# Bias bands of four heads read from one SBUF partition each instead of a copy in HBM

## The chip, the cores and the metric

The kernel runs on one core of a Trainium2 chip. The metric is the device time of one execution in microseconds (us), as the median of several runs. The core's engines work side by side, each through its own list of instructions in order: PE (matrix products, with PEld for loading weights), DVE (vector operations), ACT (exponential, copies, activations), POOL and SP. POOL and SP here mostly issue DMA transfers; each has a queue of its own, which all 16 DMA engines of the core serve (q0 in the profile is POOL's queue, q1 SP's). SBUF is the memory on the chip with 128 partitions, PSUM the one that PE writes to, HBM the memory outside.

## The reference

Attention with a relative position bias, then a feed-forward layer. There are 8 batches, 8 heads, 576 positions and 64 numbers per head:

```python
scores = scale * np.matmul(q, k.transpose(0, 1, 3, 2))
# n = abs(i - j); bucket(n) is n up to 15, then logarithmic, the last of 32 from 128 on
scores = scores + bias_table[bucket].transpose(2, 0, 1)[None]
attn = softmax(scores)
x = (attn @ v)            # to (4608, 512)
h = x @ w_in              # (512, 2048)
out = np.maximum(0.01 * h, h) @ w_out
```

The bias depends on the distance |i - j| and the head alone, and is constant from distance 128 on. A constant drops out of the softmax. So only a band of the scores about the diagonal needs the bias at all, and the kernel multiplies there by exp(bias - last bias) after the exponential.

## The kernel before

The work is cut into 32 items, one for each batch and pair of heads (`items`, n = 0 to 31; item n < 4 is pair n of batch 0). For an item, Q and K are loaded by POOL's queue, transposed (by PE for the early items), copied to SBUF by DVE or ACT (`qt`, `kt`), multiplied by PE in six parts u (`qk_mm`, scores in `ps_s`), put through the exponential by ACT (`exp`, to `at` and `at4`), multiplied by the band by DVE (`band`), multiplied with V by PE (`av...`, `ps_o`), divided and laid out for the feed-forward layer, whose products fill PE's remaining time and everything after the last item.

For the first eight items the order of all steps on all engines is written out by hand in a table, `first`, of which these lines are the start:

```python
spin 9 o, tq 0, cq 0 a, tk 0, ck 0, ap 0, spin 2 o,
begin 0, m 0 0, m 0 2, tk 1, tq 1, e 0 0, m 0 1, ck 1, e 0 2, m 0 5, e 0 1, e 0 5, m 0 4 s, m 0 3,
e 0 4, spin 3 m, cq 1 v, ap 1, e 0 3, m 1 0, tk 2, b 0 5, ck 2, b 0 1, e 1 0, m 1 1, ap 2, m 1 2,
e 1 1, b 0 0, b 0 4, m 1 4, tq 2,
begin 1, e 1 4, spin 3 m, m 1 3, b 0 2, e 1 2, b 1 0, cq 2 v, at 0, ...
```

Here `tk n` and `tq n` are PE's transposes of pair n's K and Q (L292), `ck`, `cq ... v` and `ap` DVE's copies of them (L313, L307, L299), `m n u` PE's scores of part u (L347 to L358), `e n u` ACT's exponential (L373 to L385), `b n u` DVE's band (L408, and L401 for `b 0 5`), `at n` and `ac n ...` PE's products with V, `dv` the division, and `spin` products of ones (L1041) whose result nobody reads. Each engine keeps the order of its own steps.

The band is made once, at the start. `ub` is a tile of 8 partitions, one for each head, with 512 numbers (bf16): exp(bias - last bias) laid out by distance, the same to both sides. `hk` holds for each head 128 partitions of 384 numbers, where partition i is the head's row read from number i on. That is a row fetched 128 times, shifted by one number each time. `hk4` is the same for the last 64 positions, 192 numbers wide, for all pairs. Before the change, SP stores `ub` to HBM (`u_row`, L202) and then fetches from there: heads 0 and 1, heads 2 and 3 (`load_hk`, L204), `hk4` in two halves (`load_hk4`, L211), heads 4 and 5, heads 6 and 7. Item p of batch 0 uses heads 2p and 2p + 1; `b 0 5` reads `hk`, since `hk4` comes later, and the parts 5 of all other items read `hk4`.

Of the kernel before, what the change touches and what calls it, by code (L numbers as in the profile page):

```python
# [37 lines left out]
def kernel(  # L38
# [10 lines left out]
    nc = tc.nc  # L49
# [6 lines left out]
    P = 128  # L56
# [33 lines left out]
    hk = per.tile([P, H, 3 * P], BF16, name="hk")  # L90
# [83 lines left out]
    BW = 3 * P  # L174
    ub = per.tile([H, UW], BF16, name="ub")
# [15 lines left out]
    for j, (u, lo, w, m) in enumerate(groups):  # L191
        copy = nc.scalar.copy if j % 2 else nc.vector.tensor_copy
        copy(out=ub[:, C0 + lo : C0 + lo + m * w].rearrange("h (m w) -> h m w", w=w),
             in_=e8[:, u : u + m].unsqueeze(2).to_broadcast([H, m, w]))
    row = ub[:, :]
    nc.vector.tensor_copy(
        out=ub[:, C0 - BAND + 1 : C0],
        in_=bass.AP(tensor=row.tensor, offset=row.offset + C0 + BAND - 1,
                    ap=[list(row.ap[0]), [-1, BAND - 1]]),
    )  # L200
    udr = nc.dram_tensor("u_row", [H, UW], BF16, kind="Internal")
    nc.sync.dma_start(out=udr.ap(), in_=ub)  # L202
    def load_hk(h0, h1):
        nc.sync.dma_start(  # L204
            out=hk[:, h0:h1, :],
            in_=bass.AP(tensor=udr, offset=h0 * UW, ap=[[1, P], [UW, h1 - h0], [1, BW]]),
        )

    def load_hk4(p0, p1):
        for e in range(2):  # L210
            nc.sync.dma_start(  # L211
                out=hk4[e * SL : (e + 1) * SL, p0:p1, :],
                in_=bass.AP(tensor=udr, offset=(2 * p0 + e) * UW + SL + P,
                            ap=[[1, SL], [2 * UW, p1 - p0], [1, P + SL]]),
            )

    load_hk(0, 2)
    load_hk(2, 4)
    load_hk4(0, n_pairs)
    load_hk(4, 6)  # L220
    load_hk(6, H)
# [1091 lines left out]
```

## Time and profile before

| | |
|---|---|
| median of 3 runs | 366.75 us (366.44 to 367.57) |
| the profiled execution | 365.69 us, span 363.9 us |
| PE, ACT, DVE, POOL busy | 98%, 67%, 52%, 29% of the span |
| mean granted TensorE clock | 0.995 |
| `hk` transfers, from issue to landing | 4.8 to 9.6 us, median 6.9 us |
| DVE idle until the first `hk` is there | 3.0 us, once |

The span is the time from the first instruction to the last; the execution's own time lies 1.8 us above it. Rows in order of time begin with the start in us from the span's start and the length in us. What stands in brackets is the idle time ahead of a row and what ended it. A row with x2 or more stands for several instructions in succession, some with other shapes than the first, which is the one named. Rows of a queue (SPq, POOLq, ACTq) are issues of DMAs: their length is that of the issue, not of the transfer. The rows of DMA issues end with KB each and the us from issue to landing. The rows of queues give packets, MB and the time of the packets as a share of 16 engines; packets overlap, so the share can pass 100%.

### The profile page before, as it was taken

The page shows a single profiled execution, that of the slowest core. Times are in us where ns is not written, and L with a number is a line of the kernel's source. Part 1 is how long each engine was busy: PE and PEld are TensorE (multiplying, and loading weights), DVE is VectorE, ACT ScalarE, POOL GpSimd, SP SyncE. Part 2 cuts the span into 40 slices and gives each one's busy share as a digit, 9 for nine tenths or more (in the row PEclk, how much of TensorE's full clock was granted, in tenths as well). Part 3 has the DMA queues.
Part 4 walks back from the last instruction along what each step waited for, and adds up shares of the span by engine and source line. Part 5 has one row for each costly group of instructions (what it writes and reads, how often), then busy time and mean ns, then how long its engine had stood idle before and what let it go on. Part 6 is the DMA issues. An engine that isn't in the chain of part 4 may idle for free.

```text
span 363.9 us, 12095 instructions
## 1 busy us (share of the span) xinstructions
PE 356.2 (98%) x5195; PEld 207.4 (57%) x5195; DVE 189.1 (52%) x499; ACT 243.8 (67%) x363; POOL 106.6 (29%) x195
## 2 busy tenths in 40 slices
PE   7899999999999999999999999999999999999996
PEld 3465555555557776666666666666666544444443
DVE  4698777686755767555555666556554300100000
ACT  5899987479958888777777777777776264054111
POOL 8857427253334334423343334211000000000000
PEclk9899999999999999999999999999999999999999
DMA  7999999998998899988998799765411000200212
GB/s 100 189 195 155 192 205 160 196 136 128 99 128 137 107 153 125 140 130 118 134 117 135 115 118 131 122 105 95 51 49 50 29 31 0 86 31 0 86 60 86
DMA packets 105852, 40.27 MB, mean 111 GB/s; under 512 B 83648, under 2 KB 101320, under 8 KB 105800
## 3 DMA queue, kind: packets, MB, share of 16 engines
q0 software_dynamic: 55200, 18.36, 47.9%
q1 hardware_dynamic: 49304, 19.06, 27.0%
q10 hardware_dynamic: 1296, 2.10, 1.6%
q8 instruction: 41, 0.67, 0.8%
q14 instruction: 11, 0.09, 0.1%
HBM read 37.68 MB, written 9.45 MB: 130 GB/s over the span
## 4 chain that ended last, share of the span: by engine, by line
PE 89%; POOL 2%; ACT 2%; DMA 2%; DVE 1%; issue 1%; ACTq 0%; POOLq 0%
PE pm L843 35%; PE pm L584 16%; PE pm L532 14%; PE ps_o L476 8%; PE ps_s L354 7%; PE pm L718 2%; DMA kn<-in_k_dram 2%; PE ps_o L432 1%; PE ps_o L421 1%; PE ps_s L843 1%; ACT at L373 1%; POOL vn L137 1%; PE pm L577 1%; PE ps_s L347 1%; POOL qn L124 1%
## 5 line engine op out<-in xcount | busy, mean ns | idle before, releaser
L373 ACT ACTIVATE at<-ps_s 128x1024 bf16<-128x1024 f32 x120 | 118.5, 1023 | 34.1 <-PE ps_s L354 33.3
L843 PE MATMUL pm<-xT,w_in_sb 64*128 64x512 bf16 x608 | 139.6, 376 | 0.0
L843 PE MATMUL pm<-w_out_sb,gt 64*128 64x512 bf16 x544 | 129.6, 376 | 0.0
L556 ACT ACTIVATE gt<-pm 128x512 bf16<-128x512 f32 x140 | 82.2, 606 | 39.8 <-PE pm L532 33.9
L408 DVE TENSOR_TENSOR at<-at,hk 128x768 bf16<-128x768 bf16 (+3 forms) x149 | 64.8, 452 | 35.6 <-ACT at L385 21.4
L843 PEld LDWEIGHTS <-w_in_sb 64*128 64x128 bf16 x608 | 51.9, 94 | 23.9 <-issue 1.2
L843 PEld LDWEIGHTS <-gt 64*128 64x128 bf16 x544 | 48.3, 94 | 20.8 <-issue 0.7
L584 PE MATMUL pm<-w_out_sb,gt 128*128 128x512 bf16 x268 | 59.8, 380 | 0.0
L532 PE MATMUL pm<-xT,w_in_sb 128*128 128x512 bf16 x252 | 57.8, 380 | 0.0
L354 PE MATMUL ps_s<-qt,kt 64*128 64x512 bf16 x240 | 44.9, 383 | 0.6 <-ACT at L385 0.2
L584 PEld LDWEIGHTS <-gt 128*128 128x128 bf16 x268 | 25.5, 98 | 30.2 <-DMA vn<-in_v_dram 0.4
L532 PEld LDWEIGHTS <-w_in_sb 128*128 128x128 bf16 x252 | 23.7, 98 | 26.7
L476 PEld LDWEIGHTS <-at 64*128 64x128 bf16 x1920 | 36.2, 94 | 4.1 <-issue 0.9
L476 PE MATMUL ps_o<-vn,at 64*128 64x65 bf16 x1920 | 38.5, 191 | 0.0
L131 POOL DMA_DIRECT2D vn<-in_v_dram x32 | 34.1, 1071 | 9.7 <-PE pm L843 5.2
L385 ACT ACTIVATE at<-ps_s 128x576 bf16<-128x576 f32 x30 | 19.8, 661 | 17.9 <-PE pm L843 17.9
L454 DVE TENSOR_TENSOR opair<-ps_o,rcp 128x320 bf16<-128x320 f32 x64 | 29.1, 487 | 1.1
L894 DVE COPY y<-pm 128x512 f32<-128x512 f32 x17 | 11.8, 692 | 27.7 <-PE pm L843 27.7
L1085 POOL COPY tick<-opair 1x1 bf16<-1x1 bf16 x43 | 7.9, 183 | 61.1 <-DVE opair L454 61.1
L597 DVE COPY y<-pm 128x512 f32<-128x512 f32 x11 | 7.6, 691 | 34.3 <-PE pm L584 34.2
L1085 POOL COPY tick<-at 1x1 bf16<-1x1 bf16 x21 | 5.6, 265 | 54.6 <-DVE at L408 52.3
L124 POOL DMA_DIRECT2D kn<-in_k_dram x30 | 19.5, 649 | 6.4 <-issue 6.3
(106 smaller groups left out, 341.0 us busy)
## 6 DMA issues: line engine op xcount, KB each, us to landing
out_dram<-y SPq DMA_DIRECT2D x28, 256.0 KB, 3.9
qn<-in_q_dram POOLq DMA_DIRECT2D x28, 144.0 KB, 4.6
kn<-in_k_dram POOLq DMA_DIRECT2D x28, 144.0 KB, 3.6
vn<-in_v_dram POOLq DMA_DIRECT2D x24, 128.0 KB, 4.3
w_in_sb<-in_moe_w_in_dram POOLq DMA_DIRECT2D x4, 512.0 KB, 8.9
w_out_sb<-in_moe_w_out_dram POOLq DMA_DIRECT2D x2, 1024.0 KB, 13.1
out_dram<-y ACTq DMA_DIRECT2D x7, 256.0 KB, 2.0
vn<-in_v_dram POOLq DMA_DIRECT2D x16, 64.0 KB, 7.7
```

The source lines that it names most:

```text
L124: nc.gpsimd.dma_start(out=dst[0:RQ, h0:h1, :, :].rearrange("r h c d -> r h (c d)"), in_=src[b, h0:h1, :, :].rearrange("h (r c) d -> r h (c ...
L131: nc.gpsimd.dma_start(out=vn[b % NBUF][:, c, h0:h1, 0:D], in_=v[b, h0:h1, c * P : (c + 1) * P, :].rearrange("h s d -> s h d"),)
L354: nc.tensor.matmul(ps[:, e, :], lhsT=kt[r, u * P : (u + 1) * P], rhs=qt[r, 0:512], start=True, stop=True)
L373: nc.scalar.activation(at[:, :, u, 0:512], ps, AF.Exp, scale=scale)
L385: nc.scalar.activation(at4[:, 0:w], ps.rearrange("p e i -> p (e i)")[:, 0:w], AF.Exp, scale=scale)
L408: nc.vector.tensor_tensor(out=o, in0=o, in1=m, op=ALU.mult)
L454: nc.vector.tensor_tensor(out=opair[:, 0:m, e * D : (e + 1) * D], in0=ps[:, :, 0:D], in1=rcp.to_broadcast([P, m, D]), op=ALU.mult)
L476: m = nc.tensor.matmul(outs[n][e][:, ic * (D + 1) : (ic + 1) * (D + 1)], lhsT=at[halves[r], o : o + P], rhs=vn[b % NBUF][halves[r], c, 2 * ...
L532: nc.tensor.matmul(pm, lhsT=w_in_sb[:, c, f * P : (f + 1) * P], rhs=xT[c][:, T * TT : (T + 1) * TT], start=(c == 0), stop=(c == n_cc - 1))
L556: nc.scalar.activation(g, pm, AF.Prelu, bias=0.0, scale=1.0, alpha=0.01)
L584: nc.tensor.matmul(pm, lhsT=gt[:, f, ts * P : (ts + 1) * P], rhs=w_out_sb[:, f, :], start=(f == 0), stop=(f == n_fc - 1))
L843: m = nc.tensor.matmul(o, lhsT=w, rhs=x, start=was is None, stop=need[bank] == 0)
```

## The change

Heads 0 to 3 are fetched straight from `ub` in SBUF. Each of the four is a transfer of its own: the source is one partition, read 128 times from number 0, 1, 2, ... 127 on, 384 numbers each; the target is the head's part of `hk`, as before. Heads 0 and 1 are issued ahead of the store to HBM, heads 2 and 3 behind it. `hk4` and heads 4 to 7 still come from `u_row`.

```diff
+    def turn_row(h):
+        one = ub[h : h + 1, :]
+        nc.sync.dma_start(
+            out=hk[:, h, :],
+            in_=bass.AP(tensor=one.tensor, offset=one.offset, ap=[list(one.ap[0]), [1, P], [1, BW]]),
+        )
+
+    turn_row(0)
+    turn_row(1)
     udr = nc.dram_tensor("u_row", [H, UW], BF16, kind="Internal")
     nc.sync.dma_start(out=udr.ap(), in_=ub)
...
-    load_hk(0, 2)
-    load_hk(2, 4)
+    turn_row(2)
+    turn_row(3)
     load_hk4(0, n_pairs)
     load_hk(4, 6)
     load_hk(6, H)
```

SP's list at the program's start, with what each waits for (a name ending in _49 is a semaphore; DMAHW0 to DMAHW7 are those of SP's transfers, given out in turn; hk_101 is `hk4`). Before:

```order
L202 DMA u_row<-ub 8x512 [waits DVE_49]
L204 DMA hk<-u_row 128x2x384 [waits DMAHW1_49]
L204 DMA hk<-u_row 128x2x384
L211 DMA hk_101<-u_row 64x4x192 x2
L204 DMA hk<-u_row 128x2x384 x2
```

SP's list in the changed kernel, same place:

```order
L203 DMA hk<-ub 128x1x384 [waits DVE_49]
L203 DMA hk<-ub 128x1x384
L211 DMA u_row<-ub 8x512
L203 DMA hk<-ub 128x1x384 x2
L220 DMA hk_101<-u_row 64x4x192 [waits DMAHW3_49]
L220 DMA hk_101<-u_row 64x4x192
L213 DMA hk<-u_row 128x2x384 [waits DMAHW0_49]
L213 DMA hk<-u_row 128x2x384 [waits DMAHW1_49]
```

The wait for the store to HBM (DMAHW1 before, DMAHW3 now) has moved from heads 0 and 1 to `hk4`; four single heads stand where two pairs of heads stood.

DVE's list from the last step ahead of the first band to pair 1's first parts, before (at_0_114 is `at4` of item 0, at_112 and at_113 are `at` of items 0 and 1, gt the third set of buffers, that of item 2):

```order
L299 TENSOR_TENSOR kt_111<-kt_111,own 128x128 [waits DVE_49]
L401 TENSOR_TENSOR at_0_114<-at_0_114,hk 64x192 [waits DMAHW2_49,Activation_49]
L401 TENSOR_TENSOR at_0_114<-at_0_114,hk 64x192
L313 COPY gt<-ps_t 128x576 [waits PE_49]
L408 TENSOR_TENSOR at_112<-at_112,hk 128x2x384
L299 TENSOR_TENSOR gt<-gt,own 128x128 [waits DVE_49]
L408 TENSOR_TENSOR at_112<-at_112,hk 128x2x256
L408 TENSOR_TENSOR at_112<-at_112,hk 128x2x320 [waits Activation_49]
L408 TENSOR_TENSOR at_112<-at_112,hk 128x2x384
L408 TENSOR_TENSOR at_113<-at_113,hk 128x2x256 [waits DMAHW3_49,Activation_49]
L307 COPY gt<-ps_t 128x576 [waits PE_49]
```

The same place in the changed kernel:

```order
L308 TENSOR_TENSOR kt_111<-kt_111,own 128x128 [waits DVE_49]
L410 TENSOR_TENSOR at_0_114<-at_0_114,hk 64x192 [waits DMAHW1_49,Activation_49]
L410 TENSOR_TENSOR at_0_114<-at_0_114,hk 64x192 [waits DMAHW2_49]
L322 COPY gt<-ps_t 128x576 [waits PE_49]
L417 TENSOR_TENSOR at_112<-at_112,hk 128x2x384
L308 TENSOR_TENSOR gt<-gt,own 128x128 [waits DVE_49]
L417 TENSOR_TENSOR at_112<-at_112,hk 128x2x256
L417 TENSOR_TENSOR at_112<-at_112,hk 128x2x320 [waits Activation_49]
L417 TENSOR_TENSOR at_112<-at_112,hk 128x2x384
L417 TENSOR_TENSOR at_113<-at_113,hk 128x2x256 [waits DMAHW5_49,DMAHW4_49,Activation_49]
L316 COPY gt<-ps_t 128x576 [waits PE_49]
```

No step of DVE has moved; each band now waits for its heads one by one, and lines behind the change have numbers greater by 9.

## The prediction, made before the changed kernel was run

> **What bounds the kernel now.** I read the page's busy shares first, then the stretches, then the start in order of time on each engine, then the DMA queues. On the page:
>
> ```profile
> span 363.9 us, 12095 instructions
> PE 356.2 (98%) x5195; PEld 207.4 (57%) x5195; DVE 189.1 (52%) x499; ACT 243.8 (67%) x363; POOL 106.6 (29%) x195
> ```
>
> Busy time by stretch:
>
> ```profile
> 15.00:20.00 5.00, 4.53 (x95) 2.87 (x91) 4.93 (x15) 4.77 (x8) 3.05 (x6) 1.00 1.27 225
> 20.00:25.00 5.00, 4.61 (x93) 3.12 (x91) 4.72 (x13) 4.79 (x7) 2.94 (x5) 1.00 1.64 188
> 35.00:300.00 265.00, 264.71 (x4425) 161.99 (x4421) 161.85 (x414) 196.39 (x290) 80.48 (x151) 1.00 0.86 119
> ```
>
> The columns behind the length are PE, PEld, DVE, ACT and POOL busy, then granted clock, DMA share and GB/s. From 35 to 300 us PE is busy for 264.71 of 265 us: a microsecond lost or won before that passes to the end undiminished, and no gap swallows it. The change touches only what happens before about 25 us, where PE has holes and from 15 to 25 us DVE is nearly full (4.93 and 4.72 of 5). So the question is what the change does to DVE's and PE's order there.
>
> What SP waited for (us in total, times, longest) and the issues of the bias bands on its queue, then DVE in the same place:
>
> ```profile
> SPq L204 <- DMA u_row<-ub: 3.3, 1, 3.3
> ...
> 4.57 0.28 SPq L202 DMA_DIRECT2D u_row<-ub  x1
> 8.21 0.92 SPq L204 DMA_DIRECT2D hk<-u_row  x2
> 9.17 1.34 SPq L211 DMA_DIRECT2D hk<-u_row  x2
> 10.56 1.38 SPq L204 DMA_DIRECT2D hk<-u_row  x2
> ```
> ```profile
> 9.87 0.21 DVE L299 TENSOR_TENSOR kt<-kt,own 128x128 bf16<-128x128 bf16 x1
> 13.06 0.52 DVE L401 TENSOR_TENSOR at<-at,hk 64x192 bf16<-64x192 bf16 x2 [2.98 <-DMA hk<-u_row]
> 13.82 0.76 DVE L313 COPY gt<-ps_t 128x576 bf16<-128x576 bf16 x1 [0.25 <-PE ps_t L292]
> 15.96 0.89 DVE L408 TENSOR_TENSOR at<-at,hk 128x768 bf16<-128x768 bf16 x2
> 16.77 0.75 DVE L307 COPY gt<-ps_t 128x576 bf16<-128x576 bf16 x1
> 18.93 0.25 DVE L408 TENSOR_TENSOR at<-at,hk 128x192 bf16<-128x192 bf16 x1
> 21.52 0.42 DVE L408 TENSOR_TENSOR gt<-gt,hk 128x512 bf16<-128x512 bf16 x1
> ```
>
> DVE waits 2.98 us for heads 0 and 1, the wait that the change aims at. But as soon as that step is done, DVE waits again, 0.25 us, for PE: the copy of pair 2's K at 13.82 needs PE's transposes. PE in order of time:
>
> ```profile
> 8.04 0.45 PE L292 MATMUL ps_t<-ident,kn 96*64 96x96 bf16 x12 [0.68 <-DMA kn<-in_k_dram]
> 10.72 0.51 PE L354 MATMUL ps_s<-qt,kt 64*128 64x512 bf16 x2 [0.25 <-ACT at L385]
> 11.16 1.46 PE L1041 MATMUL ps_w<-const-bfloat16-1.0 128*128 128x512 bf16 x3
> 12.55 0.61 PE L354 MATMUL ps_s<-qt,kt 64*128 64x512 bf16 x2
> 13.09 0.69 PE L292 MATMUL ps_t<-ident,kn 96*64 96x96 bf16 x12
> 17.90 0.39 PE L354 MATMUL ps_s<-gt 64*128 64x512 bf16 x2
> 18.76 0.45 PE L292 MATMUL ps_t<-ident,kn 96*64 96x96 bf16 x12 [0.47 <-DMA kn<-in_k_dram]
> ```
>
> From 10.72 to 13.78 PE runs without a gap and waits for nothing of DVE's; its chain goes back through ACT to the K load of pair 1 at 8.04. So the 2.98 us are covered by PE up to 13.82, all but nothing.
>
> **The change part by part.** Removed: the wait of SP for the copy in HBM (3.3 us) ahead of heads 0 to 3, and two issues of 192 KB. Added: four issues of 96 KB, each of 128 runs of 768 bytes, all 128 from one partition of `ub`. Bytes landed are the same, 393,216 B. Moved: the small store to HBM behind two of these, and `hk4` and heads 4 to 7 behind all four.
>
> *Earlier issue.* Heads 0 and 1 go out at 4.57 instead of 8.21. Worth 0: the cover up to 13.82 stays, since neither PE's steps nor ACT's there read `hk`.
>
> *How fast one partition can be read.* No row shows a transfer out of one partition. The rows nearest to it are stores out of SBUF on an otherwise empty DMA, which read 128 partitions evenly, and one stretch of the old fetch beside other loads:
>
> ```profile
> out_dram<-y ACTq DMA_DIRECT2D x7, 256.0 KB, 2.0
> out_dram<-y ACTq DMA_DIRECT2D x1, 64.0 KB, 1.5
> q1 hardware_dynamic: 246, 0.18, 78.6%
> q0 software_dynamic: 158, 0.02, 29.8%
> q1 hardware_dynamic: 3, 0.00, 0.9%
> ```
>
> The first two give a slope: 192 KB more in 0.5 us more, 393 GB/s for all 16 engines, 24.6 GB/s for each. The next two are 11 to 12 us: 246 runs of SP's queue (q1) in one us, so 512 would take 2.1 us. The last is 6 to 7 us, where SP's queue, issued at 4.57, has its first packets: a start of about 1.6 us. Both ends: if a partition can be read as fast as the whole memory, four heads take 2.1 us and land by 8.3. If it can give only what one sixteenth of the memory gives when all is read, a head takes 98,304 / 24.6e3 = 4.0 us, and four heads, which lie in neighbouring partitions, 16 us one after the other if they share that sixteenth. I take the second, because a store that spreads over 16 engines reached 24.6 GB/s per engine with the partitions spread too, and I see no row in which one part of SBUF gave more. The two rounded landing times leave 0.4 to 0.6 us, so 3.3 to 5.0 us for a head.
>
> The Trainium skill bears on this. Its page "SBUF — State Buffer", section "Door 1: The DMA port swizzle (why `[64,N]` ≈ `[32,N]`)", maps partitions 0 to 3 to one of 16 DMA ports and gives 27.6 GB/s as measured for them. By that figure a head takes 3.56 us and the four 14.2 us, and the sum below would come to an estimated +4.0 us instead of +5.8. No run here has shown such a port yet; the slope of the stores agrees in size.
>
> *Heads 0 and 1.* Start 6.2 plus 8.0 gives 14.2 instead of 13.06. DVE's step ends 0.5 us later, and the copy behind it starts at 14.7 instead of 13.82: 0.9 us lost, contained in the next item.
>
> *Heads 2 and 3.* 6.2 + 16 = 22.2. Their first use is pair 1's first band, second of the two steps in the row at 15.96, starting at about 16.4 (16.85 less one 0.42 step). 22.2 - 16.4 = 5.8 us. DVE runs in order: behind it stand the copy of pair 2's Q (16.77), and PE cannot do pair 2's scores (17.90) without it, nor ACT its exponentials. So this lies on the path entirely.
>
> *`u_row`, `hk4`, heads 4 to 7.* The store to HBM stands behind two heads in the same queue and lands about 14.2 + 1.7 = 16 (its 3.3 us less the start of 1.6); SP waits for it, then issues `hk4` from 16 to 17.3 and the last heads to 18.7, queued behind heads 2 and 3 (22.2). At q1's 0.18 MB per us `hk4` (two of 96 KB) needs 1.1 us and lands near 23.5 to 24. First use is at 18.93, shifted by 5.8 to 24.7: hidden, by less than a microsecond. If the shift were smaller than I say, this is late next. Heads 4 and 5 (about 25) are used at 21.52 + 5.8 = 27.3: hidden.
>
> *POOL's loads.* No instruction of its queue moves. Its packets share the engines with SP's queue earlier than before. If reads of one partition also hold up the engines, pair 1's K comes later; up to 14 us this lies within the 5.8.
>
> *Given back and lost again.* PE's wait of 0.47 at 18.76 for the last K pair ends before PE gets there: -0.5. After an idle stretch the clock falls:
>
> ```profile
> 9.50:10.00 0.50, 0.00 (x0) 0.00 (x0) 0.50 (x2) 0.50 (x1) 0.50 (x2) 1.00 1.76 113
> 10.50:11.00 0.50, 0.28 (x2) 0.09 (x1) 0.00 (x0) 0.50 (x2) 0.50 (x2) 0.87 1.08 164
> 13.50:14.00 0.50, 0.50 (x10) 0.23 (x7) 0.25 (x2) 0.50 (x1) 0.50 (x1) 0.50 1.51 167
> ```
>
> PE was idle from 9.5 to 10.0, the granted clock began to fall between 10.5 and 11.0 (0.87), and it was still 0.50 at 13.5. A stop of 5 us at 17.9 should bring another such stretch; with DVE the fuller engine there I put it at +0.3. Sum: 5.8 - 0.5 + 0.3 = +5.6 us. On the profiled execution (365.69 us, span 363.9) that is 371.3, and on the median of 366.75, 1.06 above it, 372.3. With 3.3 and 5.0 us for a head the sum runs from +2.8 to +9.6: 369.5 to 376.3.
>
> **Rivals.**
>
> *The transfers are hidden anyway.* One partition is read as fast as many. Heads 0 to 3 land at 8.3 to 10, no wait for `hk` is left, and DVE waits at 13.82 for PE instead. For it: 246 runs a microsecond came out of one 8 KB row in HBM. Against it: HBM is not SBUF. Time: 366.75 within 0.3% (1.1 us, about what a measurement here can tell from no change).
>
> *Queue share.* As before, but the 512 runs take half of the engines while the K load of pair 1 is under way:
>
> ```profile
> 3.88 0.64 POOL L124 DMA_DIRECT2D kn<-in_k_dram  x1
> ...
> kn<-in_k_dram POOLq DMA_DIRECT2D x1, 144.0 KB, 4.1
> ```
>
> It was issued at 3.88 and landed at 8.0. From 6.2 it has 1.8 us to go; sharing half for 2.4 us adds 1.2. That pushes PE's 8.04 row, ACT behind it, and so 13.82. Time: 366.75 + 1.2 = 367.95.
>
> *Faster.* The half clock from about 10.7 to 14 makes three products of ones take 1.46 us, where three at 15.09 take 0.83:
>
> ```profile
> 15.09 0.83 PE L1041 MATMUL ps_w<-const-bfloat16-1.0 128*128 128x512 bf16 x3
> ```
>
> If the earlier transfers shift PE's idle time so that the clock holds, pair 2's transposes come about 1.2 us sooner (0.6 for the products, as much again for the scores and transposes behind them), and only then does `hk` at 13.06 matter, being there early. It decides once heads 0 and 1 land before 12.4 and the clock stays at 1.00 to 13. Against it: nothing in the change gives PE more to do at 9.5. Time: 365.5.
>
> *One engine, or less than a sixteenth.* If a source with one partition is served by a single engine, 512 runs of 51 ns (78.6% of 16 us over 246) take 26 us: heads 2 and 3 land at 32.3, +15.9: 382.6. The same comes if one partition gives 15 GB/s. Against it: each transfer still has 128 target partitions. The Trainium skill's "DMA: Bandwidth & Descriptors", section "Why a DMA increments its semaphore by 16 and not by 1", lets the slowest dimension that isn't 1 set the number of engines, here 128, so 16 engines; by it this rival's first form falls. No row here has a source like it.
>
> **How the numbers follow.** A sixteenth binds: 0.43. Hidden: 0.26. Queue share: 0.09. Faster: 0.10. One engine or slower: 0.12. The forecast is the first, 372.3. Slower by over 0.3%: 0.43 + 0.09 + 0.12 = 0.64; within: 0.26; faster: 0.10. The range reaches into the faster case and leaves out half of it and the heaviest, 0.17 in all: 365.4 to 376.3. The likeliest case alone has 369.5 to 376.3.
>
> **What would show it.** Right: SP's first two issues at 4.6 with landings near 9.6 us after issue, the next two near 17; DVE idle for DMA `hk<-ub` about 1 us at the first band and 5 us at pair 1's first; PE's scores of pair 2 near 23.5; DMA GB/s low while SP's queue shows long packets (in the hundreds of ns, against 51). Wrong: landings under 6 us, DVE idle at 13.8 for PE alone, scores of pair 2 near 17.9. What would break the forecast is above all a partition that is read faster than its sixteenth; next, that heads 0 to 3 don't share one.

## The result and the profile after

| | time, median | ratio to the kernel before |
|---|---|---|
| before | 366.60 us (4 runs) | |
| changed | 377.31 us (375.4 to 378.64, 4 runs) | 1.0287, 95% interval 1.0236 to 1.0339 |

The changed kernel is 10.7 us slower, where +5.6 was forecast. The profiled execution took 377.23 us, with a span of 375.4, which is 11.5 more than before. Its page:

```profile
span 375.4 us, 12079 instructions
PE 358.2 (95%) x5177; PEld 209.6 (56%) x5195; DVE 189.1 (50%) x499; ACT 244.2 (65%) x363; POOL 106.6 (28%) x195
PEclk9687999999999999999999999999999999999999
GB/s 90 81 137 195 141 191 205 132 181 140 116 107 164 109 124 114 126 149 124 124 121 131 122 118 130 132 108 92 91 52 47 30 30 0 56 58 0 57 84 84
```

PE is busy for 2 us more and the span is 11.5 longer. The other 9.5 us are idle time of PE, most of it at the start: in the first 60 us PE is busy for 47.1 us, before for 55.4. The second slice, 9.4 to 18.8 us, moves 81 GB/s (before: 189). The page also follows back the chain of work that ended last. Its shares of the span, after and then before:

```profile
PE 80%; DMA 15%; POOL 3%; issue 1%; DVE 1%; ACT 0%; ACTq 0%; POOLq 0%
PE 89%; POOL 2%; ACT 2%; DMA 2%; DVE 1%; issue 1%; ACTq 0%; POOLq 0%
```

Nearly all of the 15% are loads of V and of weights on POOL's queue, not bands.

DVE in order of time (lines are 9 higher than before, since the change added 9):

```profile
11.72 0.25 DVE L410 TENSOR_TENSOR at<-at,hk 64x192 bf16<-64x192 bf16 x1 [1.98 <-DMA hk<-ub]
16.19 0.26 DVE L410 TENSOR_TENSOR at<-at,hk 64x192 bf16<-64x192 bf16 x1 [4.21 <-DMA hk<-ub]
17.13 0.76 DVE L322 COPY gt<-ps_t 128x576 bf16<-128x576 bf16 x1 [0.69 <-PE ps_t L301]
25.11 0.42 DVE L417 TENSOR_TENSOR at<-at,hk 128x512 bf16<-128x512 bf16 x1 [5.29 <-DMA hk<-ub]
29.46 0.26 DVE L417 TENSOR_TENSOR at<-at,hk 128x192 bf16<-128x192 bf16 x1 [1.76 <-DMA hk<-u_row]
32.06 0.41 DVE L417 TENSOR_TENSOR gt<-gt,hk 128x512 bf16<-128x512 bf16 x1
```

Four waits for bands stand where one of 2.98 stood: for head 0, for head 1, for heads 2 and 3, and for `hk4`. But pair 2's K copy (17.13) waits for PE too, and PE waits for something the change does not name. PE's rows, and POOL's issues that go with them:

```profile
7.70 0.45 PE L301 MATMUL ps_t<-ident,kn 96*64 96x96 bf16 x12 [0.31 <-DMA kn<-in_k_dram]
...
16.40 0.69 PE L301 MATMUL ps_t<-ident,kn 96*64 96x96 bf16 x12 [4.38 <-DMA kn<-in_k_dram]
26.26 0.39 PE L363 MATMUL ps_s<-gt 64*128 64x512 bf16 x2 [4.04 <-DVE gt L316]
```
```profile
11.84 0.65 POOL L124 DMA_DIRECT2D qn<-in_q_dram  x1 [1.84 <-DMA qn<-in_q_dram]
16.64 0.64 POOL L124 DMA_DIRECT2D kn<-in_k_dram  x1 [4.15 <-DMA kn<-in_k_dram]
```

Pair 2's K was issued at 5.14, at the same time as before, and PE stood 4.38 us waiting for it. POOL's queue itself stopped: the K load that it issued at 10.58 before goes out at 16.64.

The queues from 8 to 12 us, after and then before:

```profile
q1 hardware_dynamic: 167, 0.11, 65.0%
q0 software_dynamic: 256, 0.13, 23.4%
```
```profile
q0 software_dynamic: 1901, 0.37, 109.1%
q1 hardware_dynamic: 353, 0.26, 31.8%
```

SP's 167 packets took 65.0% of 64 us (4 us of 16 engines), 249 ns each, where before they took 58. POOL's queue moved 0.13 MB in place of 0.37. SP's own issues were held up, for 6.94 us in the third row:

```profile
4.57 1.23 SPq L203 DMA_DIRECT2D hk<-ub  x2
5.84 1.63 SPq L211 DMA_DIRECT2D u_row<-ub  x1
7.52 6.94 SPq L203 DMA_DIRECT2D hk<-ub  x2
17.78 4.53 SPq L220 DMA_DIRECT2D hk<-u_row  x2
22.35 1.63 SPq L213 DMA_DIRECT2D hk<-u_row  x2
```

### The profile page after: what moved, and what is told of

Read it like the earlier page. It is cut to its first block, busy times and chain, and to the rows that moved or that the text cites. A ratio compares the mean times of both kernels' runs of the same rounds, so it can differ in the third digit from the quotient of the medians.

```text
span 375.4 us, 12079 instructions
## 1 busy us (share of the span) xinstructions
PE 358.2 (95%) x5177; PEld 209.6 (56%) x5195; DVE 189.1 (50%) x499; ACT 244.2 (65%) x363; POOL 106.6 (28%) x195
## 4 chain that ended last, share of the span: by engine, by line
PE 80%; DMA 15%; POOL 3%; issue 1%; DVE 1%; ACT 0%; ACTq 0%; POOLq 0%
PE pm L852 33%; PE pm L593 15%; PE pm L541 11%; PE ps_o L485 8%; PE ps_s L363 6%; DMA vn<-in_v_dram 5%; DMA w_in_sb<-in_moe_w_in_dram 5%; DMA w_out_sb<-in_moe_w_out_dram 4%; PE pm L727 2%; PE ps_o L430 1%; PE ps_s L852 1%; POOL vn L137 1%; PE pm L586 1%; POOL kn L124 1%; POOL qn L124 1%
## 5 line engine op out<-in xcount | busy, mean ns | idle before, releaser
L593 PE MATMUL pm<-w_out_sb,gt 128*128 128x512 bf16 x261 | 59.0, 379 | 0.7 <-issue 0.5
```

The lines of the kernel that those rows point to most:

```text
L593: nc.tensor.matmul(pm, lhsT=gt[:, f, ts * P : (ts + 1) * P], rhs=w_out_sb[:, f, :], start=(f == 0), stop=(f == n_fc - 1))
```

## The experiments

Two theories after the result. P: what is slow is reading one partition many times. C: while that goes on, the DMA engines serve the two queues in turn, so POOL's loads are slowed to the same pace, and most of the loss comes by that way. Against P stands S (a source in SBUF, four transfers, or the later store to HBM); against C stands W, my own sum: only the steps that wait for the bands lose. Ratios below are to the kernel before, run beside it on the same chip, with 95% intervals.

**Source of 128 partitions instead of one.**

```diff
-        one = ub[h : h + 1, :]
...
-            in_=bass.AP(tensor=one.tensor, offset=one.offset, ap=[list(one.ap[0]), [1, P], [1, BW]]),
+            in_=wide,          # [128, 384], ones; last written where ub is
```

> The changed kernel, but the four transfers for heads 0 to 3 read a tile of 128 partitions of ones (one row of 384 numbers from each partition, not shifted) instead of one partition 128 times; same issues, same bytes, same targets; the bias of heads 0 to 3 is left out. Theory P (one partition gives only a sixteenth of what the memory gives, about 25 GB/s): the rows land within 5 us of issue, DVE no longer waits for them, time back to 366.6, within 1.1. Rival S (a source in SBUF as such, four transfers in place of two, or the store to HBM standing behind two of them, costs the time): 375 to 378, as the changed kernel.

Measured: 365.67 us, ratio 0.9991 (0.9957 to 1.0025). S falls: with the same issues, the same order and the same bytes there is no loss that can be measured (the interval ends at +0.9 us). Nor is there a gain, though heads 0 and 1 land early. DVE there:

```profile
11.45 0.54 DVE L412 TENSOR_TENSOR at<-at,hk 64x192 bf16<-64x192 bf16 x2 [0.62 <-ACT at L396]
13.36 0.76 DVE L324 COPY gt<-ps_t 128x576 bf16<-128x576 bf16 x1 [1.37 <-PE ps_t L303]
```

The first band now waits for ACT, and the copy behind it waits 1.37 us for PE: the cover that the prediction read.

**Item 0 without a band to wait for.** In the kernel before:

```diff
-        hp = hk[:, 2 * p : 2 * p + 2, :]
+        hp = hk1 if n == 0 else hk[:, 2 * p : 2 * p + 2, :]     # hk1: ones, by DVE at 4.4 us
```

> The kernel before, but item 0's bands multiply with a tile of ones that DVE fills at 4.6 us, so that the first band waits for no transfer; all transfers stay; the bias of item 0 is left out. Theory of the cover (behind the 2.98 us wait DVE waits for PE at 13.8 anyway): 366.6, within 0.5; DVE idle ahead of the copy of pair 2's K instead of ahead of the first band. Rival (the wait is on the path, what the change aims at): 363.6 to 364.5.

Measured: 365.42 us, ratio 0.9984 (0.9956 to 1.0012). The interval's lower end is a gain of 1.6 us, so the 2.1 to 3.0 us of the rival are excluded. DVE's wait has only moved, to the copy of pair 2's K:

```profile
10.48 0.52 DVE L403 TENSOR_TENSOR at<-at,hk 64x192 bf16<-64x192 bf16 x2 [0.62 <-ACT at L387]
12.39 0.76 DVE L315 COPY gt<-ps_t 128x576 bf16<-128x576 bf16 x1 [1.39 <-PE ps_t L294]
```

In these two traces the copy starts earlier than at 13.82. From 12 to 13 us the granted clock was 1.00 in both, where it was 0.50 in the trace of the kernel before. That does not hang on the bands: the kernel with unread transfers from 128 partitions, below, has 1.00 there too, with its first band's wait of 2.8 us in place.

**Transfers that nobody reads.** The kernel before, with four transfers more at the end of SP's first list; once from one partition each, once from 128 partitions:

```diff
     load_hk(6, H)
+    dmy = per.tile([P, 4, BW], BF16, name="dmy")
+    for h in range(4):
+        one = ub[h : h + 1, :]
+        nc.sync.dma_start(out=dmy[:, h, :], in_=bass.AP(tensor=one.tensor, offset=one.offset,
+                          ap=[list(one.ap[0]), [1, P], [1, BW]]))      # or in_=wide
```

> The kernel before with four transfers more, last in SP's first list (about 12 us): heads 0 to 3, each from its one partition, to a tile that nobody reads. Theory C (reads of one partition hold up the DMA engines, and POOL's loads with them): 2 to 8 us slower, 369 to 375, POOL's loads issued between 10 and 25 us land several us later, SP's packets of these rows take 200 to 500 ns. Rival W (the change costs only through the steps that wait for the bands): 366.6 to 367.7.

> As the kernel with unread transfers from one partition each, but these four read a tile of 128 partitions of ones. Theory C: only the bytes are left, 366.6 to 368. If the bytes or the four issues were the cost of the former, this is as slow as it.

Measured: 375.51 us, ratio 1.0256 (1.0213 to 1.0298), and 366.07 us, ratio 0.9992 (0.9969 to 1.0014). The loss of 9.6 us is above the range that I gave for C, and no step waits for these transfers; the bytes alone cost nothing that can be measured. So W falls: the steps that wait for bands are not the only way. The two queues from 20 to 27 us with unread transfers from one partition:

```profile
q1 hardware_dynamic: 256, 0.18, 72.3%
q0 software_dynamic: 267, 0.20, 17.9%
```

SP's queue moves 0.18 MB in 7 us, some 25 GB/s, with 256 packets of 316 ns. Counted by size in the trace, 228 of them are runs of 768 bytes (25.0 GB/s, 353 ns each) and 28 are packets of 4 bytes. POOL's queue gets 267 packets in that time, 255 of them of 768 bytes: about one for one, though its own take 75 ns each. That fits queues served in turn; the rows show the counts, not the turns. PE's and POOL's waits in this kernel:

```profile
31.53 0.69 PE L299 MATMUL ps_t<-ident,kn 96*64 96x96 bf16 x12 [4.47 <-DMA kn<-in_k_dram]
29.40 0.74 POOL L137 DMA_DIRECT2D vn<-in_v_dram  x1 [8.74 <-DMA qn<-in_q_dram]
```

**The changed kernel, with the waits for bands taken from items 0 and 1.**

```diff
-        hp = hk[:, 2 * p : 2 * p + 2, :]
+        hp = hk1 if n < 2 else hk[:, 2 * p : 2 * p + 2, :]      # and ones for hk4 of these items
```

> The changed kernel with all its transfers, but items 0 and 1 multiply with ones (a tile that DVE fills at 4.6 us), so that no step ahead of item 2 waits for a band; the bias of items 0 and 1 is left out. Theory C (while one partition is read, POOL's loads fall to the same packet rate, and PE waits for K and Q of the next pairs): little is gained, 371 to 376; PE's wait of 4.4 us for pair 2's K stays. Rival W (my prediction's sum: the steps that wait for heads 0 to 3): back to 366.6 to 368.

Measured: 374.42 us, ratio 1.0216 (1.0183 to 1.0250). Of the changed kernel's 10.7 us, 8.2 stay without any of the waits that my sum was made of (374.42 against 366.17). PE waits twice for K here, 4.24 and 4.06 us: the late loads are enough for a loss of this size. Who waited for whom in its first 45 us (us in total, times, longest; the wait for `hk` is that of item 2, for heads 4 and 5):

```profile
PE ps_t L303 <- DMA kn<-in_k_dram: 8.9, 3, 4.2
DVE gt L419 <- DMA hk<-u_row: 1.4, 1, 1.4
```

**Half of the change, one way and the other.**

```diff
     turn_row(0)
     turn_row(1)
...
-    turn_row(2)
-    turn_row(3)
+    load_hk(2, 4)
```

> Only heads 0 and 1 from their partitions, ahead of the store to HBM; heads 2 and 3 as one transfer from HBM as before the change. Theory C and P: 256 runs at 36 per us end 7 us earlier than 512, so about half of the loss: 370 to 373; heads 2 and 3 land about 20, PE's wait for pair 2's K stays near 4 us. If only heads 2 and 3 (the later wait) cost: 366.6 to 368.

```diff
-    turn_row(0)
-    turn_row(1)
...
+    load_hk(0, 2)
     turn_row(2)
     turn_row(3)
```

> Heads 0 and 1 from HBM as before the change, then heads 2 and 3 from their partitions, then the rest from HBM. Theory C and P: about half of the loss, 370 to 373; the slow stretch begins about 11 us instead of 7, pair 2's K is there in time, pair 3's K and Q and the bands of the second pair are late. If only heads 0 and 1 (ahead of the store to HBM) cost: 366.6 to 368.

Measured: heads 0 and 1 alone 373.45 us, ratio 1.0176 (1.0111 to 1.0241), with single runs from 369.6 to 374.7; heads 2 and 3 alone 372.20, ratio 1.0156 (1.0128 to 1.0183). By the ratios either half costs five to six tenths of the whole, with wide intervals (a loss of 4.1 to 8.8 us and of 4.7 to 6.7). So neither pair of heads is the cause alone. I missed a detail of the first: in its trace, which is that of the run of 369.6, pair 2's K came earlier than I wrote, and PE waited 1.40 us for it, not 4.

**Heads on partitions 0, 4, 8, ... 28.** The tiles of the row get 32 partitions, of which every fourth is used (`tabT[0:HP:4, :]`, `one = ub[4 * h : 4 * h + 1, :]`).

> The changed kernel with the eight heads' rows on partitions 0, 4, 8, ... 28 instead of 0 to 7 (the tiles of the row have 32 partitions, every fourth used). If heads 0 to 3 share one way out of SBUF, and each engine has packets of several heads under way: four ways, packets shorter, 367 to 371. If each engine goes through its packets head by head, all 16 are at one partition at a time, and placing the heads apart changes nothing: 374 to 378, packets of SP's queue 200 to 500 ns as before.

Measured: 373.41 us, ratio 1.0190 (1.0164 to 1.0215), between my two cases: a loss of 7.2 us where the changed kernel loses 10.7. Its first issue comes 0.96 us later (5.53 against 4.57), which is in the 373.41. SP's queue from 8 to 12 us:

```profile
q1 hardware_dynamic: 279, 0.19, 46.3%
```

279 packets where the changed kernel had 167, 106 ns each instead of 249 (the share of 64 us over the count). So heads 0 to 3 on neighbouring partitions do share a way out, and apart they overlap in part, 1.7 times the packets and not four times. What PE and then DVE wait for in this kernel:

```profile
19.97 0.61 PE L365 MATMUL ps_s<-gt 64*128 64x512 bf16 x2 [3.04 <-DVE gt L318]
25.28 0.43 PE L432 MATMUL ps_o<-v,at 64*128 64x65 bf16 x9 [2.33 <-DVE opair L465]
```
```profile
18.82 0.42 DVE L419 TENSOR_TENSOR at<-at,hk 128x512 bf16<-128x512 bf16 x1 [3.10 <-DMA hk<-ub]
24.34 0.26 DVE L419 TENSOR_TENSOR at<-at,hk 128x192 bf16<-128x192 bf16 x1 [2.93 <-DMA hk<-u_row]
```

PE waits for DVE's steps behind the bands of heads 2 and 3 and behind `hk4`, and for K loads only 0.2 us in all. With heads 2 and 3 alone from their partitions it is much the same: from 11 us on, PE waits 1.01 and 2.17 us for DVE and for no K load. So late bands cost several us too, without a wait of PE for POOL's loads. In the changed kernel both ways are late at once, and the losses of the two do not add: taking one away leaves most of the loss with the other. What its bands alone would cost, with POOL's loads in time, no run shows.

**Sixteen source partitions.**

```diff
-            in_=wide,
+            in_=bass.AP(tensor=wide.tensor, ..., ap=[[row, 16], [1, 8], [1, BW]]),
```

> As the kernel whose four transfers read a tile of 128 partitions of ones, but the source is 16 partitions (0 to 15) of that tile, each read 8 times, shifted by one number each time; the bias of heads 0 to 3 is left out. If a way out of SBUF serves four neighbouring partitions (0 to 3, 4 to 7, ...) and gives 28 GB/s, four of them give 112 GB/s: a head takes about 0.9 us, packets of SP's queue 60 to 150 ns, time 366 to 368. If reading a partition several times at shifted starts is slow in itself, whatever the number of partitions: 372 or more.

Measured: 366.95 us, ratio 1.0011 (0.9976 to 1.0045). From 8 to 12 us:

```profile
q1 hardware_dynamic: 547, 0.37, 35.7%
```

547 packets at 42 ns, shorter than the 60 to 150 that I expected. Shifted starts and eightfold reading do no harm that can be measured; what matters is over how many partitions the source is spread.

**Half the length, and no shift**, both on the unread transfers: `[1, BW // 2]` in place of `[1, BW]`, and `[0, P]` in place of `[1, P]`.

> As the kernel with unread transfers from one partition each, but each of the 512 runs has 192 numbers (384 bytes) instead of 384. If bytes limit (28 GB/s out of these partitions): the slow stretch is half as long, about 5 us instead of 10, 70 runs of SP's queue per us, time 369.5 to 372. If each run of such a transfer costs the same time whatever its length: 36 per us, 375 to 376.

> As the kernel with unread transfers from one partition each, but all 128 runs of a head start at the same number, so that no start is shifted. If the shifted, unaligned starts make the reads longer (up to a third more): 40 to 48 runs per us instead of 36 and 372.5 to 375. If only the bytes out of one partition count: 36 to 37 per us, 375 to 376.

Measured: half the length 368.64 us, ratio 1.0052 (1.0027 to 1.0076), a loss of 2.6 us, less than I wrote; no shift 374.67, ratio 1.0225 (1.0185 to 1.0264). Without a shift, 20 to 27 us shows again:

```profile
q1 hardware_dynamic: 256, 0.18, 70.7%
```

256 packets, as with it, and 231 runs of 768 bytes where there were 228. Unaligned starts cost nothing that this shows. From 21 to 24 us, half the length and then the whole:

```profile
q1 hardware_dynamic: 134, 0.04, 43.8%
q1 hardware_dynamic: 109, 0.07, 71.3%
```

That is 45 packets per us with half the length, against 36. I expected 70 if bytes limit and 36 if runs do; POOL's queue had 727 packets in these 3 us, against 111 with the whole length, so the two rows are not alike in the rest either. By the trace the 512 runs lie within 7.9 us instead of 13.0. Whether bytes or runs set the pace stays open. Half the bytes cost only about a quarter of the time; I take it that the start has some slack for late loads (PE waited for V, Q and K little in that kernel), but no run measured that slack by itself.

## Why the prediction was wrong in size

*The cover up to 13.82: right.* A faster arrival of heads 0 and 1 brought no gain that can be measured, twice.

*One partition gives a sixteenth: right.* I took 24.6 GB/s from the slope of the stores; some 25 was measured. The rivals "hidden" and "faster" fall with it, and "one engine", priced at 15 GB/s, too. The Trainium skill's figure of 27.6 GB/s for partitions 0 to 3 ("SBUF — State Buffer", "Door 1: The DMA port swizzle (why `[64,N]` ≈ `[32,N]`)") lies about a tenth above this case's 25. Its port map, which gives partitions 0, 4, 8 and 12 a port each, agrees with the gain from placing heads four partitions apart (279 packets against 167).

*POOL's loads: the step that failed.* I wrote that if reads of one partition hold up the engines, pair 1's K comes later and "up to 14 us this lies within the 5.8". It does not. Pair 1's K was no later (PE's row at 7.70 against 8.04), but everything loaded behind it was: the loads of the following pairs and POOL's issues. This costs 8.2 us with the bands' waits gone, and 9.6 us where nobody reads the rows at all. I had the queue share as a rival at +1.2, by taking half of the engines for 2.4 us. There was such a share (267 packets to 256 beside the unread transfers), but in the changed kernel the slow reads lasted from 7.3 to 24.0 us, not 2.4. My sum followed the bands alone, and with the two terms below it was too short there as well; in the changed kernel both ways are late.

*Heads 2 and 3: mis-sized.* 16.4 to 22.2 (+5.8) was forecast; the step starts at 25.11 (+8.7). By the trace the 512 runs lie between 7.3 and 24.0 us. They begin 1.1 us later than the 6.2 of the sum and take 16.7 us instead of 16, and the step comes 1.1 us after the last of them, for which the sum had nothing. The first bands waited 6.2 us (1.98 and 4.21), not about 1; the later wait contains that. The range of the sum has a slip: 0.4 to 0.6 us for 192 KB make 3.2 to 4.8 us for a head, not 3.3 to 5.0, and so +2.4 to +8.8. Beside POOL's small V packets SP's queue gets still less:

```profile
q0 software_dynamic: 1792, 0.26, 212.6%
q1 hardware_dynamic: 68, 0.04, 27.9%
```

These are the queues of the changed kernel from 13 to 16 us: 23 packets per us for SP. It is not one for one here: by the trace, 1660 packets of 128 bytes went by beside 50 runs of 768.

*`hk4`: wrong too.* "Hidden, by less than a microsecond" became a wait of 1.76 us at 29.46, where the step had been at 18.93: +10.5. SP's issue of `hk4` took 4.53 us instead of 1.34.

*Given back and lost again: wrong in sign.* I put -0.5 + 0.3. PE's wait of 0.47 us for the last K pair is gone (26.58, no wait), but between the band at 32.06 (before: 21.52, so +10.5) and the end (+11.5) another microsecond goes. The start has more than one stretch of low clock. Changed kernel, with the granted clock third from the end:

```profile
15.00:20.00 5.00, 3.60 (x39) 1.82 (x39) 2.91 (x7) 2.33 (x4) 3.36 (x5) 0.51 2.09 64
30.00:35.00 5.00, 4.60 (x74) 3.27 (x75) 3.99 (x11) 2.24 (x3) 3.25 (x5) 0.64 1.43 200
```

Before, both stretches had 1.00. What the clock is worth here by itself stays open: no run kept it up while the loads were late.

## What to carry to other kernels

A transfer that read one partition many times had some 25 GB/s here, about a sixteenth of the 393 GB/s from which the prediction started. Its cost was not its own delay alone. On shared engines it slowed the other queue's loads, so it must be priced by the loads that run beside it, even if nobody waits for it. Where two things are late at once, as the bands and POOL's loads were, taking one away shows what the other costs by itself, not what the first was worth. Before speeding up an arrival, look at what the waiting engine waits for next; here the first 3 us of DVE's idle time were covered by PE, and removing them changed nothing that can be measured. If a row has to be spread over all partitions, read it from HBM, or from 16 partitions, which took no measurable time more than before; what it costs to put the row on 16 partitions is not in that, since they held ones.

## What was unexpected of the hardware

Two queues on the same engines were not shared by time: 256 packets of 316 ns against 267 of 75 ns in the same 7 us. Nor were they always shared packet for packet, as 68 against 1792 from 13 to 16 us show. SP's instruction that issues a transfer was itself held up behind slow reads: two issues took 6.94 us, where the two ahead of them took 1.23 and the same two with a source of 128 partitions 1.20. A full queue would explain it; no row shows how full the queue was. Shifting the start of the runs by two bytes each made no difference to the rate (228 and 231 runs in 7 us).
